# Softmax row sums on GpSimd instead of a ones matmul, with the values product four slots behind the scores

## The chip, the cores and the metric

The kernel runs on one core of a Trainium2 chip. The metric is the device time of one execution in microseconds (us). The trace of a run covers a span about 2 us shorter than the time measured for it (372.5 against 374.23 us before).

## The reference, cut to what matters

Two independent problems A and B of the same shapes, each a query projection, grouped attention over a cache, and an output projection; all tensors are bfloat16.

```python
B, Sq, D = 16, 32, 1024
Hq, Hkv, Sk, Dh = 32, 4, 512, 128
q = (x @ wq).reshape(B, Sq, Hq, Dh)...         # 8 query heads share one k/v head
scores = einsum("bhqd,bhkd->bhqk", q, k) * Dh ** -0.5
p = softmax(scores)                            # over the 512 keys
out = einsum("bhqk,bhkd->bhqd", p, v)... @ wo
return concatenate([A, B], axis=-1)
```

## The kernel before

The attention work is 128 groups (2 problems x 16 batches x 4 k/v heads). A group has 256 query columns (8 heads x 32 positions) and 512 keys, held as four chunks of 128 on the partitions. A *slot* handles the scores of one group and the values product of an earlier one, and fills TensorE with seven matmuls ("units") of the query or output projections.

Scores come out with keys on the partitions, so the softmax denominator is a sum over partitions. The kernel before adds the four chunks on VectorE (two additions) and lets TensorE do the rest with a matrix of ones, which also puts the sum on every partition:

```python
def partial_sums(i):
    t1 = work.tile([P, 2, QW], FP32)           # P = 128, QW = 256
    nc.vector.tensor_tensor(out=t1, in0=p_sb[:, 0:2, :], in1=p_sb[:, 2:4, :], op=add)
    t = work.tile([P, QW], FP32R)
    nc.vector.tensor_tensor(out=t, in0=t1[:, 0, :], in1=t1[:, 1, :], op=add)

def values(i):
    for c in range(KC):                        # four values matmuls
        nc.tensor.matmul(ob[:, 0:QW], lhsT=v_sb[...], rhs=p_sb[:, c, :], ...)
    nc.tensor.matmul(ob[:, QW:2*QW], lhsT=ones, rhs=t)        # sum over partitions
    nc.scalar.activation(lg, ob[:, QW:2*QW], Ln)
    nc.scalar.activation(r, lg, Exp, scale=-1.0)              # 1 / sum
    # ... every fourth group: logarithms kept by a DMA

for i in range(128):                           # the slots
    scores(i)            # four matmuls, then p_sb = Exp(...) on ScalarE
    run(units, 4)
    values(i - 1)
    partial_sums(i)
    run(units, 3)
    normalize(i - 1)     # VectorE: ob * r -> oT
```

The kernel places the tiles named here in the memory called SBUF, except those that TensorE writes (`ob` and the results of the projections), which it places in the one called PSUM.

A unit ends, every eighth time, in a VectorE cast of the query projection from PSUM to `qT` (first half of the kernel), or, every 32nd time, of the output projection (second half).

Of the kernel before, what the change touches and what calls it, by code (L numbers as in the profile page):

```python
# [1 line left out]

# [5 lines left out]

BF16 = mybir.dt.bfloat16
FP32 = mybir.dt.float32  # L10
FP32R = mybir.dt.float32r
I32 = mybir.dt.int32
ACTF = mybir.ActivationFunctionType
ALU = mybir.AluOpType
AX = mybir.AxisListType

P = 128
HQ = 32
DH = 128
HKV = 4  # L20
# [2 lines left out]
SCALE = float(DH) ** -0.5  # L23

SHIFT = 44.0
ONES = 2.0 ** -75
LIMIT = 20.0


# [143 lines left out]
def kernel(  # L173
# [14 lines left out]
    nc = tc.nc  # L188
    B, SQ, D = A_x.shape
# [3 lines left out]
    KC = SK // P  # L193
# [3 lines left out]
    NH = NOUT // NW  # L197
    GRP = 4
    NG = B * HKV
    BPT = P // SQ  # L200
    QW = REP * SQ

    out_flat = out.flatten_outer_dims()
    problems = [
# [4 lines left out]
    def fast_path(ok_i):  # L209
        with ExitStack() as fctx:  # L210
            enter = fctx.enter_context
            const = enter(tc.tile_pool(name="const", bufs=1))
            blk = enter(tc.tile_pool(name="blk", bufs=20))
            kv = enter(tc.tile_pool(name="kv", bufs=2))
            work = enter(tc.tile_pool(name="work", bufs=2))
            outp = enter(tc.tile_pool(name="outp", bufs=3))
            psum = enter(tc.tile_pool(name="psum", bufs=2, space=bass.MemoryType.PSUM))
# [6 lines left out]
            nc.vector.memset(warm[:], 0.0)  # L224
            ident = const.tile([P, P], BF16, name="ident")
            make_identity(nc, ident[:])
            ones_f = const.tile([P, P], FP32, name="ones_f")
            nc.vector.memset(ones_f[:], ONES)
            ones = const.tile([P, P], FP32R, name="ones")
            nc.vector.tensor_copy(out=ones[:], in_=ones_f[:])  # L230
            one_col = const.tile([P, 1], FP32, name="one_col")
            nc.vector.memset(one_col[:], 1.0)
            shift = const.tile([P, 1], FP32, name="shift")
            nc.vector.memset(shift[:], SHIFT)
            cnt = const.tile([P, 1], FP32, name="cnt")
            nc.vector.memset(cnt[:], 0.0)
            NLR = 2 * NG // GRP
            lall = const.tile([NLR, GRP * QW], FP32, name="lall")


            def blk_tile(shape, name, dtype=BF16):
                return blk.tile(shape, dtype, name=name, tag="blk")
# [22 lines left out]
            def load_kv(j):  # L265
                pr, jj = divmod(j, NG // GRP)
                k, v = problems[pr][1], problems[pr][2]
                kT = kv.tile([P, GRP, SK], BF16, name="kT")
                v_sb = kv.tile([P, GRP, KC, DH], BF16, name="v_sb")
                if pr == 0:  # L270
                    g, b0 = divmod(jj * GRP, B)
                    ks, vs = k[b0:b0 + GRP, g], v[b0:b0 + GRP, g]
                    for q in range(GRP):
                        nc.sync.dma_start_transpose(out=kT[:, q, :], in_=ks[q])
                else:
                    ks, vs = k[jj], v[jj]
                    nc.sync.dma_start_transpose(
                        out=kT[:], in_=ks.rearrange("g k d -> (g k) d")
                    )
                nc.sync.dma_start(  # L280
                    out=v_sb[:], in_=vs.rearrange("q (p c) d -> p q c d", c=KC)
                )
                kv_tiles[j] = (kT, v_sb)
# [46 lines left out]
            def run(units, n):  # L330
                for _ in range(n):
                    next(units, None)
# [10 lines left out]
            st = {}  # L343

            def scores(i):
                pr, b, g = where(i)
                kT = kv_tiles[i // GRP][0].rearrange("p q (k c) -> p q c k", c=KC)
                s_ps = psum.tile([P, KC, QW], FP32, name="s_ps", tag="s")
                for c in range(KC):
                    nc.tensor.matmul(  # L350
                        s_ps[:, c, :],
                        lhsT=kT[:, i % GRP, c, :],
                        rhs=qT[pr, g][:, b, :, :].rearrange("p h s -> p (h s)"),
                        start=True,
                        stop=True,
                    )
                p_sb = work.tile([P, KC, QW], BF16, name="p_sb", bufs=3)
                nc.scalar.activation(  # L358
                    out=p_sb[:], in_=s_ps[:], func=ACTF.Exp, bias=shift[:], scale=SCALE
                )  # L360
                st[i] = {"p": p_sb}

            def partial_sums(i):
                p_sb = st[i]["p"]
                t1 = work.tile([P, 2, QW], FP32, name="t1")
                nc.vector.tensor_tensor(
                    out=t1[:], in0=p_sb[:, 0:2, :], in1=p_sb[:, 2:4, :], op=ALU.add
                )
                t = work.tile([P, QW], FP32R, name="t")
                nc.vector.tensor_tensor(  # L370
                    out=t[:], in0=t1[:, 0, :], in1=t1[:, 1, :], op=ALU.add
                )
                st[i]["t"] = t

            ltile = {}

            def values(i):
                d = st[i]
                v_sb = kv_tiles[i // GRP][1]
                ob = psum.tile([P, 2 * QW], FP32, name="ob", tag="ob")  # L380
                for c in range(KC):
                    nc.tensor.matmul(  # L382
                        ob[:, 0:QW],
                        lhsT=v_sb[:, i % GRP, c, :],
                        rhs=d["p"][:, c, :],
                        start=(c == 0),
                        stop=(c == KC - 1),
                    )
                nc.tensor.matmul(  # L389
                    ob[:, QW:2 * QW], lhsT=ones[:], rhs=d["t"][:], start=True, stop=True  # L390
                )
                d["ob"] = ob
                j, q = divmod(i, GRP)
                if q == 0:
                    ltile[j] = work.tile([P, GRP, QW], FP32, name="lg")
                lg = ltile[j]
                nc.scalar.activation(  # L397
                    out=lg[:, q, :], in_=ob[:, QW:2 * QW], func=ACTF.Ln
                )
                r = work.tile([P, QW], FP32, name="r")  # L400
                nc.scalar.activation(out=r[:], in_=lg[:, q, :], func=ACTF.Exp, scale=-1.0)  # L401
                d["r"] = r
                if q == GRP - 1:
                    nc.gpsimd.dma_start(  # L404
                        out=lall[j:j + 1, :],
                        in_=lg[0:1, :, :].rearrange("p q n -> p (q n)"),
                    )

            def normalize(i):
                pr, b, g = where(i)  # L410
                d = st.pop(i)
                tt, bl = divmod(b, BPT)
                if (pr, tt) not in oT:
                    oT[pr, tt] = blk_tile([P, HQ, P], "oT")
                nc.vector.scalar_tensor_tensor(  # L415
                    out=oT[pr, tt][:, g * REP:(g + 1) * REP, bl * SQ:(bl + 1) * SQ],
                    in0=d["r"][:].rearrange("p (h s) -> p h s", s=SQ),
                    scalar=ONES,
                    in1=d["ob"][:, 0:QW].rearrange("p (h s) -> p h s", s=SQ),
                    op0=ALU.mult,  # L420
                    op1=ALU.mult,
                )
# [42 lines left out]
            units = stream()  # L465
# [5 lines left out]
            def at(slot, fn, *args):  # L471
                plan.setdefault(slot, []).append((fn, args))

            for j in range(2, 2 * NG // GRP):
                at(max(0, GRP * (j - 2) + 1), load_kv, j)
            for c4 in range(3, 16):
                need = (c4 - 2) * 4 * DC / 7.0
                at(max(0, int(need) - 10), load_wq, c4 // 8, c4 % 8)
# [3 lines left out]
                nc.sync.dma_start_transpose(out=xT[1][:], in_=B_x.flatten_outer_dims())  # L482

            at(12, load_xT_b)
            for nh in range(NH):
                for hg in range(HKV):
                    at(NG - 12 + nh * 8 + hg * 2, load_wo, 0, nh, hg)
                    at(NG + 20 + nh * 18 + hg, load_wo, 1, nh, hg)

            def do_loads(i):  # L490
                for fn, args in plan.get(i, []):
                    fn(*args)


            for i in range(2 * NG):
                do_loads(i)
                scores(i)
                run(units, 4)
                if i > 0:
                    values(i - 1)  # L500
                partial_sums(i)
                run(units, 3)
                if i > 0:
                    normalize(i - 1)
            run(units, 4)
            values(2 * NG - 1)
            run(units, 4)
            normalize(2 * NG - 1)


            run(units, 8)
            sq = blk_tile([NLR, GRP * QW], "sq", FP32)
            nc.vector.tensor_tensor(out=sq[:], in0=lall[:], in1=lall[:], op=ALU.mult)
            nc.vector.tensor_scalar(
                out=sq[:], in0=sq[:], scalar1=LIMIT * LIMIT, scalar2=0.0,
# [46 lines left out]
```

## Time and profile before

| | |
|---|---|
| time, median of 4 runs | 374.01 us (371.06 to 374.36) |
| TensorE (PE) busy | 357.2 of 372.5 us, 96% |
| VectorE (DVE) busy | 243.5 us, 65% |
| GpSimd (POOL) busy | 25.1 us, 7% |
| slot, from one slot's matmuls to the next's | 2.52 us |

The page of the kernel before: the engine totals, the chain of waits by engine (the work that ended last, followed back step by step to what each step had waited for), and the groups that the change touches (busy time in us, mean ns of one).

```profile
PE 357.2 (96%) x2176; PEld 224.3 (60%) x2218; DVE 243.5 (65%) x476; ACT 248.9 (67%) x387; POOL 25.1 (7%) x53
...
PE 94%; DMA 3%; issue 1%; DVE 1%; SPq 0%
...
L397 ACT ACTIVATE lg<-ob 128x256 f32<-128x256 f32 x128 | 49.3, 385 | 39.8 <-PE ob L389 39.8
...
L401 ACT ACTIVATE r<-lg 128x256 f32<-128x256 f32 x128 | 53.7, 420 | 4.1
...
L389 PE MATMUL ob<-t,ones 128*128 128x256 f32 x128 | 46.4, 362 | 0.0
```

The chain is TensorE nearly throughout (94%), so time taken off TensorE is time taken off the kernel, as long as nothing else moves into its place. The table by stretches (stretch, length, then busy us and instructions of PE, PEld, DVE, ACT, POOL; then granted clock, DMA share, GB/s) shows how far the other engines are from doing so, in the first and the second half:

```profile
30.00:110.00 80.00, 79.47 (x501) 51.45 (x508) 64.19 (x124) 60.80 (x95) 3.55 (x7) 1.00 0.79 189
...
190.00:270.00 80.00, 79.42 (x500) 51.54 (x509) 50.88 (x102) 60.77 (x97) 7.38 (x14) 1.00 0.82 220
```

One slot in the timeline (start, length, engine, line, operation; in brackets, how long the engine had been idle and what ended that):

```profile
182.13 0.60 PE L382 MATMUL ob<-p_sb,v_sb 128*128 128x256 bf16 x4
182.49 0.36 PE L389 MATMUL ob<-t,ones 128*128 128x256 f32 x1
182.61 0.69 DVE L366 TENSOR_TENSOR t_2266<-p_sb 128x512 f32<-128x512 bf16 x1 [0.72 <-ACT p_sb L358]
182.69 0.82 PE L297 MATMUL q_ps<-xT,wq_sb 128*128 128x512 bf16 x3
183.35 0.60 PE L350 MATMUL s_ps<-qT,kT 128*128 128x256 bf16 x4
183.41 0.43 DVE L370 TENSOR_TENSOR t<-t_2266 128x256 fp32r<-128x256 f32 x1
183.75 0.68 DVE L305 CAST qT<-q_ps 128x512 bf16<-128x512 f32 x1
184.35 0.41 DVE L415 SCALAR_TENSOR_TENSOR oT<-r,ob 128x256 bf16<-128x256 f32 x1
...
185.13 0.69 DVE L366 TENSOR_TENSOR t_2298<-p_sb 128x512 f32<-128x512 bf16 x1 [0.37 <-ACT p_sb L358]
```

Values and ones matmul together take TensorE from 182.13 to 182.69, 0.56 us; four such matmuls alone take about 0.43, so the ones matmul is worth about 0.13 us a slot. Note also the two additions, 0.69 and 0.43 us: both read two tensors from SBUF.

### The profile page before, as it was taken

The numbers are of one execution on the slowest core, as the hardware profiler recorded it, in microseconds if no ns is written. First come the engines' busy times: TensorE is split into PE (matmuls) and PEld (weight loads), VectorE is DVE, ScalarE is ACT, GpSimd is POOL, SyncE is SP. The second block draws the span as 40 slices with busy tenths as digits, with TensorE's granted clock in tenths as the row PEclk, the third lists the DMA queues.
The fourth block names the chain that finished last, engine by engine and source line by source line (L and its number), as shares of the span: only waits on it lengthen the run. The fifth ranks groups of instructions, "written<-read, shape, count | busy, mean of one in ns | idle before, by whom it ended". The sixth has DMA issues, their size and how long they took to land.

```text
span 372.5 us, 6012 instructions
## 1 busy us (share of the span) xinstructions
PE 357.2 (96%) x2176; PEld 224.3 (60%) x2218; DVE 243.5 (65%) x476; ACT 248.9 (67%) x387; POOL 25.1 (7%) x53
## 2 busy tenths in 40 slices
PE   6899999999999999999999999999999999999991
PEld 3346666666666666666666666666666666666540
DVE  1247787878788788878766656766666666566530
ACT  3007777777777777777777777777777777777500
POOL 0000000000000000000001101101011110111100
PEclk9699999999999999999999999999999999999997
DMA  8992787969887877479999953489934898550000
GB/s 269 298 264 86 205 178 212 214 149 222 227 217 219 216 225 213 113 213 272 308 278 327 272 146 97 118 237 328 239 106 111 248 329 242 130 127 16 15 16 21
DMA packets 125941, 71.91 MB, mean 193 GB/s; under 512 B 74608, under 2 KB 124912, under 8 KB 125904
## 3 DMA queue, kind: packets, MB, share of 16 engines
q1 hardware_dynamic: 122080, 68.30, 69.7%
q0 software_dynamic: 1744, 2.10, 1.7%
q10 hardware_dynamic: 2080, 1.05, 0.9%
q8 instruction: 19, 0.31, 0.3%
q14 instruction: 18, 0.15, 0.1%
HBM read 51.38 MB, written 2.10 MB: 144 GB/s over the span
## 4 chain that ended last, share of the span: by engine, by line
PE 94%; DMA 3%; issue 1%; DVE 1%; SPq 0%
PE q_ps L297 30%; PE f_ps L314 30%; PE s_ps L350 15%; PE ob L382 15%; PE ob L389 4%; DMA x_sb<-in_A_x_dram 2%; DMA v_sb<-in_A_v_cache_dram 1%; SPq L428 0%; PE xT_ps L444 0%; DVE xT L448 0%; DVE qT L305 0%; DVE o_sb L323 0%; PE ok_ps L520 0%
## 5 line engine op out<-in xcount | busy, mean ns | idle before, releaser
L358 ACT ACTIVATE p_sb<-s_ps,shift 128x1024 bf16<-128x1024 f32 x128 | 142.6, 1114 | 53.3 <-PE s_ps L350 53.3
L297 PE MATMUL q_ps<-xT,wq_sb 128*128 128x512 bf16 x491 | 130.8, 386 | 2.0 <-DVE xT L448 0.9
L314 PE MATMUL f_ps<-wo_sb,oT 128*128 128x512 bf16 x491 | 129.0, 380 | 1.0
L350 PE MATMUL s_ps<-qT,kT 128*128 128x256 bf16 x512 | 76.8, 273 | 1.2 <-DVE qT L305 0.8
L382 PE MATMUL ob<-p_sb,v_sb 128*128 128x256 bf16 x512 | 76.8, 273 | 0.1
L397 ACT ACTIVATE lg<-ob 128x256 f32<-128x256 f32 x128 | 49.3, 385 | 39.8 <-PE ob L389 39.8
L350 PEld LDWEIGHTS <-kT 128*128 128x128 bf16 x512 | 56.6, 114 | 29.5 <-issue 1.0
L382 PEld LDWEIGHTS <-v_sb 128*128 128x128 bf16 x512 | 50.1, 98 | 33.1
L297 PEld LDWEIGHTS <-wq_sb 128*128 128x128 bf16 x512 | 45.5, 99 | 36.4 <-issue 4.4
L314 PEld LDWEIGHTS <-oT 128*128 128x128 bf16 x512 | 44.7, 98 | 33.0
L305 DVE CAST qT<-q_ps 128x512 bf16<-128x512 f32 x64 | 44.0, 688 | 22.9 <-PE q_ps L297 22.7
L401 ACT ACTIVATE r<-lg 128x256 f32<-128x256 f32 x128 | 53.7, 420 | 4.1
L415 DVE SCALAR_TENSOR_TENSOR oT<-r,ob 128x256 bf16<-128x256 f32 x128 | 53.4, 417 | 1.1 <-ACT r L401 1.1
L389 PE MATMUL ob<-t,ones 128*128 128x256 f32 x128 | 46.4, 362 | 0.0
L404 POOL DMA_DIRECT2D lall<-lg x32 | 15.9, 496 | 251.0 <-ACT lg L397 251.0
L389 PEld LDWEIGHTS ob<-t,ones 128*128 128x128 f32 x128 | 24.3, 190 | 1.4
L323 DVE CAST o_sb<-f_ps 128x512 bf16<-128x512 f32 x16 | 11.0, 689 | 9.9 <-PE f_ps L314 9.8
L325 POOL DMA_DIRECT2D out_dram<-o_sb x15 | 8.6, 571 | 82.2 <-DVE o_sb L323 76.3
L448 DVE COPY xT<-xT_ps 128x1024 bf16<-128x1024 bf16 x2 | 1.4, 692 | 7.3 <-PE xT_ps L444 7.3
L448 ACT COPY xT<-xT_ps 128x1024 bf16<-128x1024 bf16 x2 | 2.0, 1012 | 5.3 <-PE xT_ps L444 5.3
L444 PE MATMUL xT_ps<-ident,x_sb 128*128 128x128 bf16 x32 | 3.2, 257 | 1.8 <-DMA x_sb<-in_A_x_dram 1.8
L437 PE MATMUL warm_ps<-warm 128*128 128x512 bf16 x8 | 3.6, 631 | 1.2 <-DVE warm L224 1.2
(277 smaller groups left out, 152.3 us busy)
## 6 DMA issues: line engine op xcount, KB each, us to landing
v_sb<-in_A_v_cache_dram SPq DMA_DIRECT2D x16, 512.0 KB, 4.2
wq_sb<-in_B_wq_dram SPq DMA_DIRECT2D x8, 1024.0 KB, 7.0
wo_sb<-in_A_wo_dram SPq DMA_DIRECT2D x8, 1024.0 KB, 8.2
v_sb<-in_B_v_cache_dram SPq DMA_DIRECT2D x16, 512.0 KB, 4.0
wo_sb<-in_B_wo_dram SPq DMA_DIRECT2D x8, 1024.0 KB, 7.8
wq_sb<-in_A_wq_dram SPq DMA_DIRECT2D x7, 1024.0 KB, 7.8
out_dram<-o_sb POOLq DMA_DIRECT2D x15, 128.0 KB, 3.7
x_sb<-in_A_x_dram SPq DMA_DIRECT2D x4, 256.0 KB, 5.5
```

The lines of the kernel that those rows point to most:

```text
L297: nc.tensor.matmul(ps[:], lhsT=w[:, dc, (h % 4) * DH:(h % 4 + 1) * DH], rhs=xT[pr][:, dc, :], start=(dc == 0), stop=(dc == DC - 1),)
L305: nc.vector.tensor_copy(out=qT[pr, g][:, :, hl, :], in_=ps[:].rearrange("p (b s) -> p b s", s=SQ),)
L314: nc.tensor.matmul(ps[:], lhsT=oT[pr, tt][:, h, :], rhs=wo_tiles[pr, nh, h // REP][:, h % REP, :], start=(h == 0), stop=(h == HQ - 1),)
L323: nc.vector.tensor_copy(out=o_sb[:], in_=ps[:])
L350: nc.tensor.matmul(s_ps[:, c, :], lhsT=kT[:, i % GRP, c, :], rhs=qT[pr, g][:, b, :, :].rearrange("p h s -> p (h s)"), start=True, stop=True,)
L358: nc.scalar.activation(out=p_sb[:], in_=s_ps[:], func=ACTF.Exp, bias=shift[:], scale=SCALE)
L382: nc.tensor.matmul(ob[:, 0:QW], lhsT=v_sb[:, i % GRP, c, :], rhs=d["p"][:, c, :], start=(c == 0), stop=(c == KC - 1),)
L389: nc.tensor.matmul(ob[:, QW:2 * QW], lhsT=ones[:], rhs=d["t"][:], start=True, stop=True)
L397: nc.scalar.activation(out=lg[:, q, :], in_=ob[:, QW:2 * QW], func=ACTF.Ln)
L401: nc.scalar.activation(out=r[:], in_=lg[:, q, :], func=ACTF.Exp, scale=-1.0)
L404: nc.gpsimd.dma_start(out=lall[j:j + 1, :], in_=lg[0:1, :, :].rearrange("p q n -> p (q n)"),)
L415: nc.vector.scalar_tensor_tensor(out=oT[pr, tt][:, g * REP:(g + 1) * REP, bl * SQ:(bl + 1) * SQ], in0=d["r"][:].rearrange("p (h s) -> p h ...
```

## The change

The ones matmul goes. GpSimd's sum across partitions (`partition_all_reduce`) does that step, for two groups at once, and to give it time the values product runs four slots behind the scores. Logarithm and exponential also cover two groups. The VectorE additions stay as they are. One slot in four runs a projection matmul less; these are saved for the four extra slots at the end. The output-weight and cache loads are planned anew.

```diff
-            LAG (one slot)
+    LAG = 4
             def partial_sums(i):
...
-                t = work.tile([P, QW], FP32R, name="t")
+                j, q = divmod(i, 2)
+                if q == 0:
+                    tsum[j] = work.tile([P, 2, QW], FP32, name="t")
                 nc.vector.tensor_tensor(
-                    out=t[:], in0=t1[:, 0, :], in1=t1[:, 1, :], op=ALU.add
+                    out=tsum[j][:, q, :], in0=t1[:, 0, :], in1=t1[:, 1, :], op=ALU.add
                 )
+                if q == 1:
+                    sums[j] = work.tile([P, 2, QW], FP32, name="sums", bufs=3)
+                    nc.gpsimd.partition_all_reduce(
+                        sums[j][:].rearrange("p q n -> p (q n)"),
+                        tsum.pop(j)[:].rearrange("p q n -> p (q n)"),
+                        channels=P, reduce_op=bass_isa.ReduceOp.add)
+            def reciprocals(j):
+                lg = sums.pop(j)
+                nc.scalar.activation(out=lg[:], in_=lg[:], func=ACTF.Ln, scale=DOWN)
+                rcp[j] = work.tile([P, 2, QW], FP32, name="r")
+                nc.scalar.activation(out=rcp[j][:], in_=lg[:], func=ACTF.Exp, scale=-1.0)
             def values(i):
...
-                nc.tensor.matmul(
-                    ob[:, QW:2 * QW], lhsT=ones[:], rhs=d["t"][:], start=True, stop=True
-                )
...
+            for i in range(total_slots + LAG):
+                scores(i)
+                if i % 2 == 1 and i >= 3: reciprocals(i // 2 - 1)   # logs kept by a DMA
+                run(units, 4 if live else 5)
+                if i >= LAG: values(i - LAG)
+                if live: partial_sums(i)
+                run(units, 3 - (i % 4 == 3) if live else 3)
+                if i >= LAG: normalize(i - LAG)
```

(Cuts are marked with "..."; the first two lines and the slot loop are condensed.)

More of the change, by code (lines that the diff above doesn't have):

```diff
@@ L4 @@
 import concourse.tile as tile
-from concourse import bass_utils, mybir
+from concourse import bass_isa, bass_utils, mybir
 from concourse._compat import with_exitstack
@@ L25 @@
 SHIFT = 44.0
-ONES = 2.0 ** -75
+DOWN = 2.0 ** -75
 LIMIT = 20.0
@@ L212, in fast_path @@
             const = enter(tc.tile_pool(name="const", bufs=1))
-            blk = enter(tc.tile_pool(name="blk", bufs=20))
+            blk = enter(tc.tile_pool(name="blk", bufs=19))
             kv = enter(tc.tile_pool(name="kv", bufs=2))
@@ L226, in fast_path @@
             make_identity(nc, ident[:])
-            ones_f = const.tile([P, P], FP32, name="ones_f")
-            nc.vector.memset(ones_f[:], ONES)
-            ones = const.tile([P, P], FP32R, name="ones")
-            nc.vector.tensor_copy(out=ones[:], in_=ones_f[:])
             one_col = const.tile([P, 1], FP32, name="one_col")
@@ L236, in fast_path @@
             nc.vector.memset(cnt[:], 0.0)
-            NLR = 2 * NG // GRP
-            lall = const.tile([NLR, GRP * QW], FP32, name="lall")
+            NLR = NG
+            lall = const.tile([NLR, 2 * QW], FP32, name="lall")
             def blk_tile(shape, name, dtype=BF16):
@@ L268, in load_kv @@
                 kT = kv.tile([P, GRP, SK], BF16, name="kT")
-                v_sb = kv.tile([P, GRP, KC, DH], BF16, name="v_sb")
+                v_sb = kv.tile([P, GRP, KC, DH], BF16, name="v_sb", bufs=3)
                 if pr == 0:
@@ L356, in scores @@
                     )
-                p_sb = work.tile([P, KC, QW], BF16, name="p_sb", bufs=3)
+                p_sb = work.tile([P, KC, QW], BF16, name="p_sb", bufs=LAG + 2)
                 nc.scalar.activation(
@@ L361, in scores @@
                 st[i] = {"p": p_sb}
+            tsum, sums, logs, rcp = {}, {}, {}, {}
             def partial_sums(i):
                 p_sb = st[i]["p"]
-                t1 = work.tile([P, 2, QW], FP32, name="t1")
+                t1 = work.tile([P, 2, QW], FP32, name="t1", bufs=1)
                 nc.vector.tensor_tensor(
@@ L368, in partial_sums, with keep_logs @@
                 )
-                t = work.tile([P, QW], FP32R, name="t")
+                j, q = divmod(i, 2)
+                if q == 0:
+                    tsum[j] = work.tile([P, 2, QW], FP32, name="t")
                 nc.vector.tensor_tensor(
-                    out=t[:], in0=t1[:, 0, :], in1=t1[:, 1, :], op=ALU.add
+                    out=tsum[j][:, q, :], in0=t1[:, 0, :], in1=t1[:, 1, :], op=ALU.add
                 )
-                st[i]["t"] = t
-            ltile = {}
+                if q == 1:
[3 more added lines that the diff above has]
+                        tsum.pop(j)[:].rearrange("p q n -> p (q n)"),
+                        channels=P,
+                        reduce_op=bass_isa.ReduceOp.add,
+                    )
+            def reciprocals(j):
[3 more added lines that the diff above has]
+                nc.scalar.activation(out=rcp[j][:], in_=lg[:], func=ACTF.Exp, scale=-1.0)
+                logs[j] = lg
+            def keep_logs(j):
+                nc.scalar.dma_start(
+                    out=lall[j:j + 1, :],
+                    in_=logs.pop(j)[0:1, :, :].rearrange("p q n -> p (q n)"),
+                )
             def values(i):
-                d = st[i]
                 v_sb = kv_tiles[i // GRP][1]
-                ob = psum.tile([P, 2 * QW], FP32, name="ob", tag="ob")
+                ob = psum.tile([P, QW], FP32, name="ob", tag="ob")
                 for c in range(KC):
                     nc.tensor.matmul(
-                        ob[:, 0:QW],
+                        ob[:],
                         lhsT=v_sb[:, i % GRP, c, :],
-                        rhs=d["p"][:, c, :],
+                        rhs=st[i]["p"][:, c, :],
                         start=(c == 0),
@@ L388, in values @@
                     )
-                nc.tensor.matmul(
-                    ob[:, QW:2 * QW], lhsT=ones[:], rhs=d["t"][:], start=True, stop=True
-                )
-                d["ob"] = ob
-                j, q = divmod(i, GRP)
-                if q == 0:
-                    ltile[j] = work.tile([P, GRP, QW], FP32, name="lg")
-                lg = ltile[j]
-                nc.scalar.activation(
-                    out=lg[:, q, :], in_=ob[:, QW:2 * QW], func=ACTF.Ln
-                )
-                r = work.tile([P, QW], FP32, name="r")
-                nc.scalar.activation(out=r[:], in_=lg[:, q, :], func=ACTF.Exp, scale=-1.0)
-                d["r"] = r
-                if q == GRP - 1:
-                    nc.gpsimd.dma_start(
-                        out=lall[j:j + 1, :],
-                        in_=lg[0:1, :, :].rearrange("p q n -> p (q n)"),
-                    )
+                st[i]["ob"] = ob
             def normalize(i):
@@ L416, in normalize @@
                     out=oT[pr, tt][:, g * REP:(g + 1) * REP, bl * SQ:(bl + 1) * SQ],
-                    in0=d["r"][:].rearrange("p (h s) -> p h s", s=SQ),
-                    scalar=ONES,
-                    in1=d["ob"][:, 0:QW].rearrange("p (h s) -> p h s", s=SQ),
+                    in0=rcp[i // 2][:, i % 2, :].rearrange("p (h s) -> p h s", s=SQ),
+                    scalar=DOWN,
+                    in1=d["ob"][:].rearrange("p (h s) -> p h s", s=SQ),
                     op0=ALU.mult,
@@ L474, in fast_path @@
             for j in range(2, 2 * NG // GRP):
-                at(max(0, GRP * (j - 2) + 1), load_kv, j)
+                at(GRP * (j - 1), load_kv, j)
             for c4 in range(3, 16):
@@ L484, in fast_path @@
             at(12, load_xT_b)
-            for nh in range(NH):
-                for hg in range(HKV):
-                    at(NG - 12 + nh * 8 + hg * 2, load_wo, 0, nh, hg)
-                    at(NG + 20 + nh * 18 + hg, load_wo, 1, nh, hg)
+            for hg in range(HKV):
+                at(52 + 2 * hg, load_wo, 0, 0, hg)
+                at(68 + 4 * hg, load_wo, 0, 1, hg)
+                at(85 + 4 * hg, load_wo, 1, 0, hg)
+                at(104 + 2 * hg, load_wo, 1, 1, hg)
             def do_loads(i):
@@ L492, in do_loads @@
                     fn(*args)
-            for i in range(2 * NG):
-                do_loads(i)
-                scores(i)
-                run(units, 4)
-                if i > 0:
-                    values(i - 1)
-                partial_sums(i)
-                run(units, 3)
-                if i > 0:
-                    normalize(i - 1)
-            run(units, 4)
-            values(2 * NG - 1)
-            run(units, 4)
-            normalize(2 * NG - 1)
+            total_slots = 2 * NG
+            for i in range(total_slots + LAG):
+                live = i < total_slots
+                if live:
+                    do_loads(i)
+                    scores(i)
+                if i % 2 == 1 and i >= 3:
+                    if i >= 5:
+                        keep_logs(i // 2 - 2)
+                    if i // 2 - 1 < NG:
+                        reciprocals(i // 2 - 1)
+                run(units, 4 if live else 5)
+                if i >= LAG:
+                    values(i - LAG)
+                if live:
+                    partial_sums(i)
+                run(units, 3 - (i % 4 == 3) if live else 3)
+                if i >= LAG:
+                    normalize(i - LAG)
             run(units, 8)
-            sq = blk_tile([NLR, GRP * QW], "sq", FP32)
+            sq = blk_tile([NLR, 2 * QW], "sq", FP32)
             nc.vector.tensor_tensor(out=sq[:], in0=lall[:], in1=lall[:], op=ALU.mult)
```

## The prediction

> **What bounds the kernel now.** TensorE. The engine totals give PE 357.2 of 372.5 us (96%); the chain of waits is 94% PE. In the table by stretches, 30 to 350 us, PE is busy 79.4 of every 80 us at full granted clock, VectorE 64 (first half) or 51, ScalarE 61, GpSimd 4 to 8. The timeline shows a slot (one group of 128) every 2.52 us. By starts of matmuls it splits into 0.86 us (four projection matmuls), 0.56 (four values and the ones matmul), 0.66 (three projection) and 0.44 (four scores). Four values matmuls alone should take 0.43 like the scores, so the ones matmul costs TensorE about 0.13 us a slot; the chain gives it 4.0%, 0.116 us. [...]
>
> **Removed.** 128 ones matmuls and weight loads on the critical engine: 128 x 0.116 to 0.13 = 15 to 17 us. ScalarE: two operations on 256 columns a slot (0.385 + 0.420 us) become two on 512 columns every second slot. I estimate 0.63 us each (slope of its listed operations), so 0.63 us a slot instead of 0.81. ScalarE's queue also issues 64 small log DMAs (before, GpSimd issued 32).
>
> **Added.** 64 sums across partitions of 128x512 on GpSimd. No trace before has one. [...] the change's plan only makes sense if one fits within two slots. [...] 2 x 2.39 = 4.8 us available. The results are wanted about 3.3 us after the sum starts, but two scores buffers and the four-slot lag absorb another slot. VectorE's work stays: two additions (0.69 + 0.42), normalization (0.41), casts.
>
> **The danger.** [...] Both additions have two SBUF inputs: 1.1 us a slot. In the first half VectorE needs 2.02 us of a 2.39 us slot, so it can lose only 0.37 us a slot before it becomes the bottleneck; in the second half 0.8 us. No run here shows the size. [...] I expect part only.
>
> **Tail and head.** The four extra slots are filled with projection work saved from earlier slots, so the tail stays about equal. The GpSimd routine's first use may cost some us.
>
> **Predicted.** 373.9 - 16 + about 1 = 359 us. Range 353 to 385, skewed upward. Chances: faster by over 2% 0.68, within 2% 0.14, slower 0.18.
>
> **What would show it.** Right: slot near 2.39 us between successive score exponentials; PE still above 95%; [...] the logarithm hardly waiting; additions still 0.69 and 0.42 us. Wrong on contention: the additions lengthen, or VectorE sits idle before them, more in the first half. Wrong on the sum's length: GpSimd near 100%, the logarithm waits for it, and scores wait for exponentials.
>
> **What would make it wrong.** A sum over 4.8 us; [...] GpSimd's output DMAs queued behind sums; reordered output-weight loads arriving late.

Passages are cut from this text where they said of the hardware what no trace showed: a remark on the ones matmul's listed time, an estimate of the sum's length with what rested on it (GpSimd's expected busy share, the time if additions waited for whole sums), and the sentences on why an addition should wait for GpSimd. The danger is the expectation that VectorE's additions lose time beside GpSimd's sum ("part only": for part of a sum). The forecast's sum came to 373.9 - 16 + about 1 = 359 us. The 16 is worked out from the trace before (128 times 0.116 to 0.13 us); the "about 1" is an allowance that comes from no trace and is not broken down.

## The result, and the profile after

403.29 us, median of 4 runs (402.05 to 403.87), against 374.01 us: the ratio is 1.080 (95% interval 1.074 to 1.086). The change made the kernel 29.3 us slower, where 15 us less had been predicted. All ratios here are the mean time of one kernel's runs over the mean of the other's of the same rounds, so they are not quite the ratio of the medians that are quoted.

The page after: engine totals, chain of waits by engine, and the sum and the logarithm.

```profile
PE 352.7 (88%) x2090; PEld 210.9 (53%) x2090; DVE 328.5 (82%) x474; ACT 216.7 (54%) x259; POOL 215.9 (54%) x85
...
DVE 35%; POOL 19%; PE 19%; ACT 17%; issue 7%; DMA 1%; POOLq 0%; DVEq 0%
...
L376 POOL PARTITION_ALL_REDUCE sums<-t x64 | 207.4, 3241 | 143.1 <-DVE t L371 79.8
...
L385 ACT ACTIVATE sums<-sums 128x512 f32<-128x512 f32 x64 | 40.4, 632 | 103.9 <-POOL sums L376 95.6
```

The sum takes 3.24 us, well inside two slots (2 x 2.52 us before), and GpSimd is busy only 54% of the span. TensorE is no longer the chain. VectorE's busy time rose by 85 us although the change gave it no work. The stretches show it near saturation in the first half:

```profile
110.00:190.00 80.00, 70.62 (x434) 43.60 (x432) 77.95 (x111) 48.17 (x58) 48.20 (x15) 1.00 0.71 188
...
270.00:350.00 80.00, 75.97 (x468) 46.86 (x466) 71.73 (x101) 51.69 (x63) 54.51 (x22) 1.00 0.72 203
```

The time of the first addition alone, over the whole span, first before and then after (stretch, length, busy time and count, clock, DMA share, GB/s):

```profile
0.00:372.50 372.50, 88.38 (x128) 0.98 0.73 193
```

```profile
0.00:401.20 401.20, 185.48 (x128) 0.98 0.65 179
```

The same 128 instructions hold VectorE 97 us longer. The timeline shows which of them, and when:

```profile
181.51 3.23 POOL L376 PARTITION_ALL_REDUCE sums<-t  x1 [2.33 <-ACT p_sb L355]
...
182.11 2.19 DVE L365 TENSOR_TENSOR t_1882<-p_sb 128x512 f32<-128x512 bf16 x1
...
184.41 0.42 DVE L371 TENSOR_TENSOR t<-t_1882 128x256 f32<-128x256 f32 x1
184.75 0.42 DVE L415 SCALAR_TENSOR_TENSOR oT<-r,ob 128x256 bf16<-128x256 f32 x1
184.78 0.63 ACT L385 ACTIVATE sums<-sums 128x512 f32<-128x512 f32 x1 [1.48 <-POOL sums L376]
...
185.08 0.69 DVE L302 CAST qT<-q_ps 128x512 bf16<-128x512 f32 x1
...
185.68 0.68 DVE L365 TENSOR_TENSOR t_1911<-p_sb 128x512 f32<-128x512 bf16 x1
...
186.40 0.42 DVE L371 TENSOR_TENSOR t<-t_1911 128x256 f32<-128x256 f32 x1
...
187.08 3.23 POOL L376 PARTITION_ALL_REDUCE sums<-t  x1 [2.33 <-ACT p_sb L355]
187.11 2.75 DVE L365 TENSOR_TENSOR t_1945<-p_sb 128x512 f32<-128x512 bf16 x1
```

Read it with the end of each addition in mind. The sum starts at 181.51; the addition that starts 0.60 us later ends at 184.30, 2.79 us after the sum's start. The next sum starts at 187.08; the addition that starts 0.03 us later ends at 189.86, 2.78 us after it. Of the 63 first additions that follow a sum, 62 end 2.77 to 2.80 us after the sum's start, whether they began 0.02 or 1.44 us after it. An addition by itself takes 0.68 us, so each of them stood still until 2.10 us after the sum's start and then ran. In the one remaining case the addition began 0.02 us *before* the sum:

```profile
327.57 3.76 POOL L376 PARTITION_ALL_REDUCE sums<-t  x1 [0.80 <-DVE t L371]
...
327.55 0.68 DVE L365 TENSOR_TENSOR t_3499<-p_sb 128x512 f32<-128x512 bf16 x1
328.34 2.28 DVE L371 TENSOR_TENSOR t<-t_3499 128x256 f32<-128x256 f32 x1
```

Here the addition took its 0.68 us and the sum waited: it took 3.76 us instead of 3.23. The second addition then stood still in its place, 2.28 us instead of 0.42. Only one addition of this run starts more than 2.1 us into a sum that is still running (at 3.30 us); it ran undisturbed, in 0.68 us, as did two that start at 2.39 us in run e8_pair_order below.

The timeline also shows why the next sum is late. From its release at 2.10 us VectorE has, one after another, the first addition, the second (L371), a normalization (L415), often a cast (L302), and the two additions of the next group; then the next sum can start, and the next standing still with it. Here that loop takes 5.57 us; where no cast lies in it, 4.96. Two slots of matmuls take less: 4.67 us in run e3_write_only below.

A second loss stands at the start. Lines of the timeline after, for GpSimd and TensorE: the second of the two instructions that build the identity matrix, and the transposes that wait for it.

```profile
11.79 0.28 POOL masks.py:199 TENSOR_SCALAR_AFFINE_SELECT ident<-ident 128x128 bf16<-128x128 bf16 x1 [10.86 <-issue]
12.13 1.86 PE L444 MATMUL xT_ps<-ident,x_sb 128*128 128x128 bf16 x16 [7.35 <-POOL ident masks.py:199]
```

Before, the same select ran at 1.03 us. The first projection matmul begins at 17.52 us instead of 10.42.

### The profile page after: what moved, and what is told of

It reads as the page before. It is cut to its first block, busy times and chain, and to the rows that moved or that the text cites. A ratio compares the mean times of both kernels' runs of the same rounds, so it can differ in the third digit from the quotient of the medians.

```text
span 401.2 us, 5820 instructions
## 1 busy us (share of the span) xinstructions
PE 352.7 (88%) x2090; PEld 210.9 (53%) x2090; DVE 328.5 (82%) x474; ACT 216.7 (54%) x259; POOL 215.9 (54%) x85
## 3 DMA queue, kind: packets, MB, share of 16 engines
q10 hardware_dynamic: 4128, 1.18, 1.6%
## 4 chain that ended last, share of the span: by engine, by line
DVE 35%; POOL 19%; PE 19%; ACT 17%; issue 7%; DMA 1%; POOLq 0%; DVEq 0%
POOL sums L376 19%; PE q_ps L294 9%; ACT p_sb L355 8%; DVE t L371 6%; PE f_ps L311 5%; ACT r L387 5%; ACT sums L385 4%; DVE qT L302 3%; PE ob L400 2%; DVE oT L415 2%; PE s_ps L347 2%; PE xT_ps L444 1%; DVE t_3096 L365 1%; DVE t_1152 L365 1%; DVE t_1945 L365 1%
## 5 line engine op out<-in xcount | busy, mean ns | idle before, releaser
L376 POOL PARTITION_ALL_REDUCE sums<-t x64 | 207.4, 3241 | 143.1 <-DVE t L371 79.8
L355 ACT ACTIVATE p_sb<-s_ps,shift 128x1024 bf16<-128x1024 f32 x128 | 138.2, 1105 | 41.3 <-PE s_ps L347 41.2
L294 PE MATMUL q_ps<-xT,wq_sb 128*128 128x512 bf16 x512 | 136.1, 384 | 18.8 <-DVE qT L302 17.9
L311 PE MATMUL f_ps<-wo_sb,oT 128*128 128x512 bf16 x512 | 131.6, 379 | 0.5 <-DVE qT L302 0.5
L385 ACT ACTIVATE sums<-sums 128x512 f32<-128x512 f32 x64 | 40.4, 632 | 103.9 <-POOL sums L376 95.6
L294 PEld LDWEIGHTS <-wq_sb 128*128 128x128 bf16 x512 | 50.5, 99 | 47.5 <-issue 17.5
L311 PEld LDWEIGHTS <-oT 128*128 128x128 bf16 x512 | 50.0, 98 | 33.1 <-issue 0.8
L415 DVE SCALAR_TENSOR_TENSOR oT<-r,ob 128x256 bf16<-128x256 f32 x128 | 52.9, 414 | 3.2 <-ACT r L387 2.6
L302 DVE CAST qT<-q_ps 128x512 bf16<-128x512 f32 x64 | 43.9, 685 | 11.7 <-PE q_ps L294 11.7
L387 ACT ACTIVATE r<-sums 128x512 f32<-128x512 f32 x64 | 40.4, 632 | 2.0
L444 PEld LDWEIGHTS <-x_sb 128*128 128x128 bf16 x32 | 3.4, 144 | 9.1 <-issue 8.8
```

Source lines behind the costliest of these rows:

```text
L294: nc.tensor.matmul(ps[:], lhsT=w[:, dc, (h % 4) * DH:(h % 4 + 1) * DH], rhs=xT[pr][:, dc, :], start=(dc == 0), stop=(dc == DC - 1),)
L302: nc.vector.tensor_copy(out=qT[pr, g][:, :, hl, :], in_=ps[:].rearrange("p (b s) -> p b s", s=SQ),)
L311: nc.tensor.matmul(ps[:], lhsT=oT[pr, tt][:, h, :], rhs=wo_tiles[pr, nh, h // REP][:, h % REP, :], start=(h == 0), stop=(h == HQ - 1),)
L355: nc.scalar.activation(out=p_sb[:], in_=s_ps[:], func=ACTF.Exp, bias=shift[:], scale=SCALE)
L376: nc.gpsimd.partition_all_reduce(sums[j][:].rearrange("p q n -> p (q n)"), tsum.pop(j)[:].rearrange("p q n -> p (q n)"), channels=P, reduc ...
L385: nc.scalar.activation(out=lg[:], in_=lg[:], func=ACTF.Ln, scale=DOWN)
```

## The experiments

The theory: (a) *read contention*: an addition with two SBUF inputs stands still while a GpSimd sum reads, and in this order of work the standing still lies in a loop on VectorE that is longer than two slots; (b) *two libraries*: the identity waits for a GpSimd library. The rival for (a): the *latency* of the path through sum, logarithm and exponential, which ScalarE's 95.6 us of waiting for GpSimd in the page after seems to show. A further rival: VectorE's sheer load.

### e1_one_input: the additions with one SBUF input

```diff
-                nc.vector.tensor_tensor(out=t1[:], in0=p_sb[:, 0:2, :], in1=p_sb[:, 2:4, :], op=ALU.add)
-                nc.vector.tensor_tensor(out=tsum[j][:, q, :], in0=t1[:, 0, :], in1=t1[:, 1, :], op=ALU.add)
+                nc.vector.tensor_reduce(out=tsum[j][:, q, :],
+                    in_=p_sb[:].rearrange("p c n -> p n c"), axis=AX.X, op=ALU.add)
```

> The changed kernel with one edit: the two additions of a group (two SBUF inputs each) become one tensor_reduce over the four key chunks (one SBUF input). Theory 'read contention' (VectorE's two-input additions stand still while a GpSimd sum reads): the reduction takes about 1.2 us and is never stretched, VectorE's busy time falls from 328 us to about 250, slot near 2.37 us, time about 366 us (359 plus about 7 for the late identity). Rival 'latency' (the sum's 3.2 us plus logarithm and exponential hold up ScalarE and normalization whatever VectorE does): stays near 400 us.

Measured: 401.25 us (before beside it 374.05), results right. Taken by itself this looks like the rival's win. The page of this run says otherwise:

```profile
L367 DVE TENSOR_REDUCE t<-p_sb 128x256 f32<-128x1024 bf16 x128 | 247.8, 1936 | 16.0 <-ACT p_sb L355 16.0
```

All 128 reductions take between 1.88 and 1.96 us, whether a sum is under way or not: with one input nothing stands still. But a reduction costs 1.94 us and not the 1.2 us of my expectation, a guess that no trace gave, against 1.11 us for the two undisturbed additions, and that adds 106 us of VectorE work (128 x 0.83), about what the standing still had cost. The half of the expectation about contention held; the time says nothing between the theories, because the substitute was as dear as the fault.

### e2_library: one GpSimd library

The trace of the changed kernel holds two pairs of GpSimd's instruction MODIFY_POOL_CONFIG, one just before the select of the identity (0.95 us) and one at the sum's line (12.30 us). With the edit below one pair is left, at the line of `load_library` (0.82 us). So I take each pair for the load of a library; and as the results are right, the sum's library serves the select too.

```diff
+            nc.gpsimd.load_library(library_config._reserved_1)
             make_identity(nc, ident[:])
```

> The changed kernel with one edit: the GpSimd library that holds the sum is loaded explicitly before the identity is built, so that one library serves both and no other is loaded for the identity. Theory 'two libraries': in the changed kernel the identity's second instruction began at 11.8 us (1.0 before) because another library was loaded for it; here it begins at about 1 us and the time falls by about 7 us, to about 396. Rival (the load itself costs this, whichever it is): still begins near 11 us, time near 403.

Measured: 392.72 us (ratio to before 1.050), 10.6 us less than the changed kernel's median. The timeline for GpSimd:

```profile
1.18 0.29 POOL masks.py:199 TENSOR_SCALAR_AFFINE_SELECT ident<-ident 128x128 bf16<-128x128 bf16 x1
```

The first sum starts at 31.20 us instead of 39.65, so 8.4 us of the gain lies before it, out of 9.0 between the two traces. Part (b) holds as far as this: with the sum's library loaded first the select starts at 1.18 us and not at 11.79. Why the select was late in the changed kernel, when the kernel before makes it after one such pair at 1.03 us, no run here shows.

### e3_write_only: GpSimd works as long, but only writes

The sum is replaced by seven memsets: one column of `t`, so that GpSimd waits for the additions as the sum does, then the whole of `sums` six times.

```diff
-                    nc.gpsimd.partition_all_reduce(sums[j], tsum.pop(j), channels=P, reduce_op=add)
+                    nc.gpsimd.memset(tsum.pop(j)[:, 1, 0:1], 0.0)
+                    for _ in range(6):
+                        nc.gpsimd.memset(sums[j][:], 2.0 ** 75)
```

> Wrong results on purpose. The changed kernel with the sum replaced by GpSimd work of about the same length that only writes: one column of t (so that it waits for the additions as the sum does) and then the whole of sums six times. Both additions keep two SBUF inputs; everything downstream still waits for GpSimd. 'Read contention': additions back to 0.69 and 0.42 us, time about 358 to 360 us (no library load either). 'Latency': if the writes take about 3.2 us in all, still near 395 to 400. 'Any GpSimd access blocks': additions stretched as in the changed kernel.

Measured: 355.90 us, ratio to before 0.952. The page:

```profile
L378 POOL MEMSET sums<- 128x512 f32 x384 | 201.8, 525 | 20.6 <-DMA lall<-sums 1.6
...
L365 DVE TENSOR_TENSOR t<-p_sb 128x512 f32<-128x512 bf16 x128 | 88.2, 689 | 63.3 <-ACT p_sb L355 62.4
```

GpSimd's work is as long as the sum (six memsets took 3.44 us in the timeline), its place in the chain of dependences is the same, the additions still have two inputs, and they take 0.69 us. So the latency of the path is not what costs, and GpSimd's writing does not disturb. It also gives the size of the intended gain: 18 us below before.

### e4_both: e1_one_input and e2_library together

> e1_one_input and e2_library together: right results. 'Read contention' and 'two libraries' together: about 358 us, faster than both kernels, PE at least 94% busy. If one of them is wrong: 366 or more.

Measured: 392.04 us, the same as e2_library, for the reason found in e1_one_input: the reduction takes 1.94 us.

### e5_per_group: a sum for every group, half as long

The same additions, the same number of columns summed, in 128 sums of 256 columns each instead of 64 of 512; library as in e2_library.

```diff
-                if q == 1:
+                if q == 0:
                     sums[j] = work.tile([P, 2, QW], FP32, name="sums", bufs=3)
-                    nc.gpsimd.partition_all_reduce(sums[j][...], tsum.pop(j)[...], ...)   # 512 columns
+                nc.gpsimd.partition_all_reduce(sums[j][:, q, :], tsum[j][:, q, :], ...)   # 256 columns
```

> e2_library with one more edit: a sum across partitions for every group as soon as its two additions are done (128 sums of 128x256) in place of one for two groups (64 of 128x512). Right results. 'Read contention': in the changed kernel the first addition after a sum ends 2.78 us after the sum's start in nearly every pair, which leaves 2.1 us of standing still; if that is the time in which the sum reads 512 columns, 256 columns read for about 1.1 us, while the next first addition is due 1.0 to 1.3 us after the sum's start. Additions then mean at most about 0.9 us instead of 1.45, a sum takes 1.7 to 2 us, time 356 to 368 us. If the standing still has a fixed length of 2.1 us whatever the columns: twice as many blocks, slower than e2_library's 392.7 us, above 420.

Measured: 357.92 us (356.32 to 359.24), ratio to before 0.959 (0.953 to 0.965), results right. This version beats both kernels. The page (the chain of waits first, now TensorE again) and two lines of the timelines of GpSimd and VectorE:

```profile
PE 72%; DVE 11%; DMA 5%; ACT 3%; POOL 2%; issue 2%; SPq 2%; ACTq 0%; DVEq 0%
...
L377 POOL PARTITION_ALL_REDUCE sums<-t x128 | 230.1, 1801 | 91.2 <-DVE t L372 64.0
...
L366 DVE TENSOR_TENSOR t<-p_sb 128x512 f32<-128x512 bf16 x128 | 135.7, 1060 | 20.2 <-ACT p_sb L356 19.3
```

```profile
121.83 1.79 POOL L377 PARTITION_ALL_REDUCE sums<-t  x1 [0.53 <-issue]
```

```profile
122.53 0.95 DVE L366 TENSOR_TENSOR t<-p_sb 128x512 f32<-128x512 bf16 x1
```

The addition ends 1.65 us after the sum's start; 1.63 to 1.65 us is the usual value in this run. Less the 0.68 us of the addition, it was released 0.96 us after the sum's start. So the standing still goes with the columns: 2.10 us for 512, 0.96 for 256. The blocks are not gone: the additions still mean 1.06 us (I expected at most 0.9), 47 us in all above 0.69. But now the loop from one sum to the next (0.96 us of standing still, two additions of 1.11, a handoff of 0.1 to 0.2) is about 2.2 us, shorter than a slot, and normalization and cast fall into the time in which the additions could not run anyway. Two slots take 4.68 us on average (from first to last score exponential), against 5.25 in the changed kernel and 5.03 before. (Against before, some 0.11 us of this is no gain but an estimate of the work moved to the end: half a projection matmul in two slots, at 0.86 us for four.)

### e6_read_copies: does only the sum disturb, or any reading?

e3_write_only with four copies of `t` into `sums` in place of the memsets; wrong results on purpose.

```diff
-                    nc.gpsimd.memset(...)                      # seven of them
+                    for _ in range(4):
+                        nc.gpsimd.tensor_copy(out=sums[j][:], in_=src[:])
```

> Wrong results on purpose. e3_write_only with its writes replaced by four GpSimd copies of t into sums (128x512, they read and write). 'Read contention' (not something peculiar to the sum): additions that meet the copies are stretched, mean of the first addition over 1.0 us against 0.69 in e3_write_only, and the time lies above e3_write_only's 355.9 us, by how much depends on the copies' length. If only the sum across partitions blocks: additions stay 0.69 us, about 356 us.

Measured: 360.39 us, ratio to before 0.962. The page:

```profile
L378 POOL COPY sums<-t 128x512 f32<-128x512 f32 x256 | 183.5, 717 | 136.3 <-ACT r L384 59.6
...
L365 DVE TENSOR_TENSOR t<-p_sb 128x512 f32<-128x512 bf16 x128 | 101.2, 790 | 43.1 <-ACT p_sb L355 42.6
...
L371 DVE TENSOR_TENSOR t<-t 128x256 f32<-128x256 f32 x128 | 67.9, 531 | 9.1 <-DVE t L365 0.5
```

Both additions are stretched (0.79 and 0.53 us against 0.69 and 0.425 in e3_write_only), 26 us in all, by ordinary copies. So it is GpSimd's reading, not something peculiar to the sum. My number was too high (over 1.0 us). A copy that meets no addition takes 0.61 us; the first additions stand still for 0.42 us at most, and the copy behind such an addition mostly takes 0.95 us. So each waits for the other, and additions get in between two copies, while a sum holds one off for 2.1 us in one piece.

### e7_half_casts: less load on VectorE

e2_library with every second cast to `qT`, from the ninth on, on ScalarE.

```diff
-                        nc.vector.tensor_copy(
+                        (nc.scalar.copy if h % 2 and h >= REP else nc.vector.tensor_copy)(
```

> e2_library with one more edit: every second cast of the projection's result to qT (from the ninth on) is made by ScalarE instead of VectorE. Right results. If the blocking costs time because VectorE's own work plus 1.5 us of standing still in every second slot exceeds two slots (VectorE is the bottleneck), 28 casts of 0.69 us taken off VectorE shorten the time by 10 to 19 us from 392.7 us, all in the first half. If the latency of the single blocked addition is what counts (chain addition, sum, logarithm, exponential, normalization), no change or slower.

Measured: 387.29 us, 5.4 us below e2_library (by medians of different rounds), less than the 10 to 19 expected; 24 casts moved, not the 28 I had counted. The sums' spacing says what happened. Of the first 31 intervals between sums, 26 were longer than 5.3 us (with a cast in the loop) in e2_library and 15 here: 11 times 0.60 us is 6.6 us. The other casts had been running in the 2.1 us in which the additions stood still, and were free. So load as such is not the cause; what counts is what stands in the loop after the release.

### e8_pair_order: the same instructions in another order on VectorE

e2_library, but the additions of both groups of a pair are made one after the other just before their sum. Number and length of sums, VectorE's instructions and the results are unchanged.

```diff
-                if live:
+                if live and i % 2 == 1:
+                    partial_sums(i - 1)
                     partial_sums(i)
```

> e2_library with one more edit: VectorE makes the additions of both groups of a pair one after the other, just before their sum, instead of one group's additions in each slot. Same instructions, same 64 sums of 128x512, right results; only the order on VectorE differs, so that normalizations and casts (about 2 us a pair) follow each sum's start and the next additions come later. 'Read contention in a serial loop' (sum's start, 2.1 us of standing still, then additions, normalization, additions, next sum: 4.96 us, with a cast 5.56 us, against 4.7 us for two slots): nearly no addition stands still, first addition 0.69 to 0.8 us on average, sums 4.7 us apart, time 355 to 361 us. If the count of sums or their length or VectorE's load is the cause, whatever the order: near e2_library's 392.7 us.

Measured: 367.69 us, ratio to before 0.985 (0.978 to 0.991), so whether it is 2% faster than before stays unclear; 25 us below e2_library (by medians of different rounds). Page and timeline:

```profile
DVE 46%; PE 19%; POOL 13%; ACT 9%; issue 7%; DMA 2%; DVEq 1%; ACTq 0%; SPq 0%; POOLq 0%
...
L366 DVE TENSOR_TENSOR t<-p_sb 128x512 f32<-128x512 bf16 x128 | 148.2, 1158 | 13.6 <-ACT p_sb L356 6.9
```

```profile
125.65 1.21 DVE L366 TENSOR_TENSOR t<-p_sb 128x512 f32<-128x512 bf16 x1
126.97 0.43 DVE L372 TENSOR_TENSOR t<-t 128x256 f32<-128x256 f32 x1
127.50 0.69 DVE L366 TENSOR_TENSOR t<-p_sb 128x512 f32<-128x512 bf16 x1
128.22 0.42 DVE L372 TENSOR_TENSOR t<-t 128x256 f32<-128x256 f32 x1
```

Order alone is worth 25 us, so neither the number of sums, nor their length, nor VectorE's load makes the loss by itself; and ScalarE waits for GpSimd as long as before (93.6 us), so that wait was a symptom. My expectation was half right: the time fell, but not to 355 to 361 us. Nearly every first addition after a sum still meets it (mean 1.16 us, expected at most 0.8): VectorE finishes its other work and comes to the next addition mostly 0.75 to 1.6 us after the sum's start, too early. The loop now holds only the release at 2.10 us, the four additions of a pair (2.22 us) and handoffs, and the sums are 4.83 us apart in most intervals; two slots of matmuls need 4.67. It is still the loop that sets the pace, but by a little.

### e5_again: e5_per_group beside e8_pair_order on one chip

> The same kernel as e5_per_group, beside e8_pair_order on one chip, to see which of the two is the better version: e5_per_group again near 358 us (0.96 of before); e8_pair_order equal or up to 2 us faster, as fewer additions stand still.

Measured: 360.00 us (ratio 0.964), against 367.69 for e8_pair_order. The expected order of the two was wrong: half-length sums beat the reordering. The reason I see is that they bring the loop below a slot; the chain of waits fits it, with TensorE at 83% here and at 19% in e8_pair_order.

| run | time, us | ratio to before | standing still of the first additions |
|---|---|---|---|
| changed kernel | 403.29 | 1.080 | 97 us |
| e1_one_input | 401.25 | 1.073 | none, but a 1.94 us reduction |
| e2_library | 392.72 | 1.050 | 97 us |
| e4_both | 392.04 | 1.050 | none, but a 1.94 us reduction |
| e7_half_casts | 387.29 | 1.036 | 95 us |
| e8_pair_order | 367.69 | 0.985 | 60 us |
| e6_read_copies (wrong results) | 360.39 | 0.962 | 13 us, and 14 in the second |
| e5_per_group | 357.92 and 360.00 | 0.959 and 0.964 | 47 and 45 us |
| e3_write_only (wrong results) | 355.90 | 0.952 | none |

(The last column is busy time of the first addition less 128 x 0.69 us; for e7_half_casts, the excess of its 62 stretched additions.)

## Why the prediction was wrong

**What bounds the kernel, and the intended gain.** Right. With the disturbance away (e3_write_only) the kernel takes 355.9 us, 18 us below before; 15 to 17 were predicted for the ones matmuls, and about as much came (this run holds the whole change but the sum itself, so it does not measure the ones matmuls alone).

**The length of the sum.** 3.24 us measured. That a sum fits into two slots (4.8 us available by the prediction, 4.67 us in e3_write_only) was not the question.

**The danger was named, and its size was the step that failed.** The prediction said that VectorE "can lose only 0.37 us a slot before it becomes the bottleneck" and then "I expect part only". Its sum, 373.9 - 16 + about 1, holds at most that 1 us for the standing still, which measured 36.8 us (e2_library less e3_write_only). Part it was: 2.10 us of a 3.23 us sum. But nearly every sum was met, 62 of 63, and an addition lost about 1.6 us each time, 0.76 us a slot: twice what the prediction itself had allowed in the first half. I gave the case in which this tips over a chance of 0.18 although the budget stood in the same paragraph, and nothing in the text estimated the loss. From the plan alone it could have been seen that the next addition comes 1.0 to 1.3 us after the sum's start (in the trace before, 183.84 to 185.13 us) and would meet any block longer than that.

**A bound by load was the wrong form.** The prediction compared VectorE's load with a slot. What formed is a loop: sum starts, addition stands still until 2.10 us, additions, normalization, perhaps a cast, additions, next sum: 4.96 or 5.57 us against 4.67 for two slots. This is why VectorE is not at 100% and yet sets the pace, why the second half, for which I had allowed 0.8 us a slot, lost time as well, and why moving casts away gave little (e7_half_casts) and reordering gave 25 us (e8_pair_order).

**First use of the GpSimd routine "may cost some us".** Named, with the same 1 us at most in the sum; it cost 10.6 us by medians (8.4 in the traces up to the first sum). The mechanism was sharper than I thought: it delayed the identity matrix (select at 11.79 us instead of 1.03), for which TensorE waits at the very start.

**The sum of the parts.** -18.1 us (e3_write_only against before beside it) + 36.8 (e2_library less e3_write_only: reading) + 10.6 (changed kernel less e2_library: library) = +29.3 us; measured +29.3. These differences add up by construction, so that is no check. The middle term can be had a second way, which is one: two slots take 5.25 us in the changed kernel and 4.67 in e3_write_only, 0.58 us on 63.5 pairs, 36.8 us.

**What stays open.** In 29 of the 64 sums the trace names a score exponential on ScalarE as the releaser. The second addition ends 0.25 to 0.28 us before the sum's start in 59 of the 64, whichever engine is named, so I read that addition as what releases them; no run tests this alone. Nor does any run show why the identity's select came 10.8 us late in the changed kernel and not in the one before.

## What to carry to other kernels

Before moving work to an idle engine, test how long the busy engine's instructions take beside the new work: GpSimd at 7% was idle, but VectorE's additions with two SBUF inputs, 0.69 us beside GpSimd's memsets and 0.79 us beside its copies, stood still for 2.10 us beside a sum of 512 columns and 0.96 us beside one of 256. Cut such instructions short enough that the loop of standing still plus the work between two of them fits into the slot (e5_per_group, 0.96 of before), rather than batch them; and when an instruction's mean grows without a change of shape, plot the *ends* of the long ones against the other engine's starts. Load the library of a GpSimd routine such as this sum before anything on GpSimd that TensorE waits for: that was worth 10.6 us here (e2_library).
